# Recutting the last 128 tokens of a fused SSM and feed-forward kernel: pieces of 256, 128 and 128 columns against 416 and 96

## Chip, cores, metric

The kernel runs on one core of one Trainium2 chip. The metric is device time in microseconds, as the median of several executions.

## The reference, cut to what matters

```python
xn = layernorm(x)                          # x: 2048 tokens x 512, bf16
h  = scan over tokens of a diagonal complex SSM driven by xn
y  = x + 2*Re(h @ C.T) + xn*Dskip + (silu(xn @ w_gate) * (xn @ w_up)) @ w_down
```

The last matmuls into y contract over 1376 feed-forward rows and over the real and imaginary parts of 512 SSM states. In the kernel these are 19 passes of up to 128 rows into one PSUM bank for each block of 128 tokens.

## The kernel before

The 2048 tokens are four chunks of 512, each four blocks ("lt") of 128 tokens. For each block, ten passes of the feed-forward product (A) and nine more (B: one of left-over feed-forward rows, eight of SSM states, tile `hss`) gather in a PSUM bank. VectorE then adds the residual held in `x_sb`, and SyncE issues a store. Instructions are recorded as tasks with what they read and write. TensorE keeps the program's order; VectorE's order is chosen by a list scheduler that goes by the length of what depends on a task.

```python
def dc_chunk(c, mid=None, split_last=False):
    items = []
    for lt in range(4):
        if split_last and lt == 3:         # only in the last chunk
            items += [(lt, 0, 256), (lt, 256, 128), (lt, 384, 128)]
        else:
            items.append((lt, 0, 512))
    prs = [next_pair() for _ in range((len(items) + 1) // 2)]   # pairs of PSUM banks, 4 in all
    for (lt, c0, nc_), bk in zip(items, banks):
        ...                                # A: 10 matmuls of nc_ columns, hT x wd
    for (lt, c0, nc_), bk in zip(items, banks):
        ...                                # B: 9 matmuls of nc_ columns, hL x wd and hss x W12
        ...                                # VectorE: x_sb[:, a, c0:c0+nc_] += pbank[:, bk, 0:nc_]
        if nc_ == 128 and c0 == 256:
            continue
        d0, dn = (256, 256) if nc_ == 128 else (c0, nc_)
        dma(..., out_v[:, a, d0:d0 + dn], x_sb[:, a, d0:d0 + dn], ...)
```

## Time and profile before

| | before |
|---|---|
| three runs, us | 178.62, 179.29, 179.01 |
| span of the profiled run, us | 177.02 |
| TensorE busy, its share of the chain | 98%, 98% |
| VectorE busy | 92% |

In the profile lines, PE is TensorE, PEld its weight loads, DVE VectorE, SPq and ACTq the issues of stores by SyncE and ScalarE; xN counts the instructions in a line, and what stands behind <- ended the wait before them. The chain is the work that ended last, followed back from the end. A store lands when its completion is signalled.

The second is VectorE's order in that stretch (timeline: start, length, what, and how many):

```profile
161.71 1.28 DVE L985 TENSOR_TENSOR x_sb<-pb,x_sb 128x512 bf16<-128x512 f32 x2
162.90 2.36 DVE L914 TENSOR_TENSOR hss<-rot 128x2048 bf16<-128x2048 bf16 x2
165.17 1.23 DVE L612 TENSOR_TENSOR xn_sb<-xn_sb,dsk 128x2048 bf16<-128x2048 bf16 x1
```

Two adds of the chunk before stand ahead of the last writes of `hss`, which the last chunk's B needs.

### The profile page before, as it was taken

The numbers are of one execution on the slowest core, as the hardware profiler recorded it, in microseconds if no ns is written. First come the engines' busy times: TensorE is split into PE (matmuls) and PEld (weight loads), VectorE is DVE, ScalarE is ACT, GpSimd is POOL, SyncE is SP. The second block draws the span as 40 slices with busy tenths as digits, with TensorE's granted clock in tenths as the row PEclk, the third lists the DMA queues.
The fourth block names the chain that finished last, engine by engine and source line by source line (L and its number), as shares of the span: only waits on it lengthen the run. The fifth ranks groups of instructions, "written<-read, shape, count | busy, mean of one in ns | idle before, by whom it ended". The sixth has DMA issues, their size and how long they took to land.

```text
span 177.0 us, 2416 instructions
## 1 busy us (share of the span) xinstructions
PE 173.3 (98%) x927; PEld 84.0 (47%) x935; DVE 162.8 (92%) x283; ACT 87.4 (49%) x116; POOL 11.0 (6%) x22
## 2 busy tenths in 40 slices
PE   8999999999999999999999999999999999999994
PEld 3894444444444444444444444444444444444644
DVE  2975999899999999999999999999999999999943
ACT  4689989989999579220455554000366520000000
POOL 3040500055000000000000000000000000000000
DMA  5891694755675200002000000001100000000032
GB/s 167 280 373 61 142 126 104 252 120 118 118 255 140 46 0 0 0 4 89 31 0 0 0 0 4 0 0 59 59 0 4 0 0 0 0 0 33 30 111 67
DMA packets 22966, 12.37 MB, mean 70 GB/s; under 512 B 15180, under 2 KB 22956, under 8 KB 22956
## 3 DMA queue, kind: packets, MB, share of 16 engines
q1 hardware_dynamic: 22652, 11.77, 24.7%
q10 hardware_dynamic: 304, 0.46, 0.8%
q8 instruction: 7, 0.11, 0.3%
q14 instruction: 3, 0.02, 0.0%
HBM read 6.46 MB, written 2.10 MB: 48 GB/s over the span
## 4 chain that ended last, share of the span: by engine, by line
PE 98%; issue 0%; DVE 0%
PE pb L762 36%; PE pb L966 19%; PE pb L883 16%; PE pb L980 16%; PE pb L806 4%; PE pb L478 3%; PE pb L977 2%; PE pb L845 2%; PE pb L855 1%; PE pb L585 1%; DVE x_sb L985 0%
## 5 line engine op out<-in xcount | busy, mean ns | idle before, releaser
L923 DVE TENSOR_TENSOR_SCAN rot<-sm,car,rot 128x512 bf16<-128x512 f32 x32 | 38.7, 1266 | 0.0
L774 ACT ACTIVATE sg<-pb 128x1024 bf16<-128x1024 f32 x20 | 20.1, 1023 | 32.7 <-PE pb L762 32.0
L966 PE MATMUL pb<-wd,hT 128*128 128x512 bf16 (+2 forms) x176 | 34.5, 355 | 0.3 <-ACT uf L870 0.2
L980 PE MATMUL pb<-W,hss 128*128 128x512 bf16 (+2 forms) x140 | 29.6, 354 | 0.2
L762 PE MATMUL pb<-xnT,wu 128*128 128x512 bf16 x120 | 27.9, 379 | 0.0
L966 PEld LDWEIGHTS pb<-wd,hT 128*128 128x128 bf16 x180 | 16.8, 98 | 18.2 <-issue 0.4
L832 ACT ACTIVATE uf<-pb 128x1024 bf16<-128x1024 f32 x20 | 20.5, 1025 | 7.7 <-PE pb L762 7.4
L762 PE MATMUL pb<-xnT,wg 128*128 128x512 bf16 x92 | 21.8, 380 | 0.0
L883 PE MATMUL pb<-xnT,BT 128*128 128x512 bf16 x96 | 21.0, 379 | 0.0
L980 PEld LDWEIGHTS pb<-W,hss 128*128 128x128 bf16 x144 | 13.4, 97 | 14.4
L890 ACT ACTIVATE u_sb<-pb 128x1024 bf16<-128x1024 f32 x16 | 16.3, 1018 | 5.2 <-PE pb L883 5.2
L762 PEld LDWEIGHTS pb<-xnT,wu 128*128 128x128 bf16 x120 | 11.7, 98 | 14.2 <-ACT sg L774 0.2
L883 PEld LDWEIGHTS pb<-xnT,BT 128*128 128x128 bf16 x96 | 9.4, 98 | 11.3
L985 DVE TENSOR_TENSOR x_sb<-pb,x_sb 128x512 bf16<-128x512 f32 (+2 forms) x18 | 11.1, 630 | 3.7 <-PE pb L980 3.0
L762 PEld LDWEIGHTS pb<-xnT,wg 128*128 128x128 bf16 x92 | 9.0, 98 | 10.6
L834 DVE TENSOR_TENSOR hT<-sg,uf 128x1024 bf16<-128x1024 bf16 x20 | 13.4, 680 | 0.4 <-ACT uf L832 0.3
L483 DVE BATCH_NORM_STATS2 st<-x_sb 128x6 f32<-128x512 bf16 x12 | 7.5, 680 | 2.7 <-DMA x_sb<-in_A_x_dram 2.7
L914 DVE TENSOR_TENSOR rot<-u_sb,cosT 128x2048 bf16<-128x2048 bf16 x8 | 9.8, 1219 | 0.0
L914 DVE TENSOR_TENSOR rot<-rot,sin 128x2048 bf16<-128x2048 bf16 x8 | 9.8, 1219 | 0.0
L914 DVE TENSOR_TENSOR rot<-u_sb,sin 128x2048 bf16<-128x2048 bf16 x8 | 9.7, 1217 | 0.0
L914 DVE TENSOR_TENSOR rot<-rot,cosT 128x2048 bf16<-128x2048 bf16 x8 | 9.7, 1215 | 0.0
L914 DVE TENSOR_TENSOR rot<-rot 128x2048 bf16<-128x2048 bf16 x8 | 9.6, 1219 | 0.0
(93 smaller groups left out, 180.7 us busy)
## 6 DMA issues: line engine op xcount, KB each, us to landing
out_dram<-x_sb SPq DMA_DIRECT2D x15, 128.0 KB, 1.7
x_sb<-in_A_x_dram SPq DMA_DIRECT2D x3, 512.0 KB, 4.5
wd<-in_B_w_down_dram SPq DMA_DIRECT2D x1, 1280.0 KB, 6.2
wu<-in_B_w_up_dram SPq DMA_DIRECT2D x1, 768.0 KB, 4.7
wu<-in_B_w_up_dram SPq DMA_DIRECT2D x1, 608.0 KB, 6.8
x_sb<-in_A_x_dram SPq DMA_DIRECT2D x4, 128.0 KB, 3.2
wg<-in_B_w_gate_dram SPq DMA_DIRECT2D x1, 480.0 KB, 5.6
wg<-in_B_w_gate_dram ACTq DMA_DIRECT2D x1, 448.0 KB, 3.8
```

The source lines that it names most:

```text
L483: return g.add("dve", lambda e, a=a: e.bn_stats(out=st[:, a % 8, :], in_=x_sb[:, a, :]), reads=[("x", a)], writes=[("st", a % 8), ("st0", ...
L762: inst = e.matmul(pbank[0:fs, bk, :].rearrange("p (j t) -> p j t", j=4), lhsT=w[:, kt, i * 128:i * 128 + fs], rhs=xnT[c][:, :, kt, :], sta ...
L774: g.add("act", lambda e: e.activation(out=sg[rows, sl, 0:n, :].rearrange("p a t -> p (a t)"), in_=pair_f32(rows, bk, 512 * n), func=AF.Sil ...
L832: g.add("act", lambda e: e.activation(out=uf[rows, ul, 0:n, :].rearrange("p a t -> p (a t)"), in_=pair_f32(rows, bk, 512 * n), func=AF.Ide ...
L834: g.add("dve", lambda e: e.tensor_tensor(out=hT[rows, hb, i0:i0 + n, :], in0=sg[rows, sl, 0:n, :], in1=uf[rows, ul, 0:n, :], op=ALU.mult), ...
L883: inst = e.matmul(pbank[:, bk, :].rearrange("p (j t) -> p j t", j=4), lhsT=BT[:, ri, kt, pt * 128:(pt + 1) * 128], rhs=xnT[c][:, :, kt, :] ...
L890: g.add("act", lambda e: e.activation(out=u_sb[:, us].rearrange("p r t -> p (r t)"), in_=pair_f32(slice(0, 128), b0), func=AF.Identity), r ...
L914: tt = lambda out, a, b, op, r, w, nm: g.add("dve", lambda e: e.tensor_tensor(out=out, in0=a, in1=b, op=op), reads=r, writes=w, name="%s_% ...
L923: g.add("dve", lambda e, A0=A0, A1=A1, k=k, ri=ri, pt=pt: e.tensor_tensor_scan(out=A1[:, k, ri, :], data0=rr[:, pt:pt + 1].to_broadcast([1 ...
L966: inst = e.matmul(pbank[:, bk, 0:nc_], lhsT=hT[0:fs, hb, i, lt * 128:(lt + 1) * 128], rhs=wd[0:fs, i, c0:c0 + nc_], start=(i == 0), stop=F ...
L980: inst = e.matmul(pbank[:, bk, 0:nc_], lhsT=hss[:, hb, pt, ri, lt * 128:(lt + 1) * 128], rhs=W12[:, ri, pt, c0:c0 + nc_], start=False, sto ...
L985: g.add("dve", lambda e, bk=bk, a=a, c0=c0, nc_=nc_: e.tensor_tensor(out=x_sb[:, a, c0:c0 + nc_], in0=pbank[:, bk, 0:nc_], in1=x_sb[:, a, ...
```

## The change

The intent: what comes after the last matmul (an add, a store, its completion) can't be hidden, so make the last piece small, and put enough matmul work behind the big piece to cover its own add and store. The diff, cut to its core (it also drops the argument `mid`):

```diff
-                    items.append((lt, 0, 256))
-                    items.append((lt, 256, 128))
-                    items.append((lt, 384, 128))
+                    items.append((lt, 0, 416))
+                    items.append((lt, 416, 96))
...
-            for (lt, c0, nc_), bk in zip(items, banks):
+            def add_A(lt, c0, nc_, bk):
                 def mmA(e, ...):           # unchanged
...
+            for it, bk in zip(items, banks):
+                if it[2] >= 256:
+                    add_A(*it, bk)
             for (lt, c0, nc_), bk in zip(items, banks):
                 a = 4 * c + lt
+                if nc_ < 256:
+                    add_A(lt, c0, nc_, bk)
...
-                if nc_ == 128 and c0 == 256:
-                    continue
-                d0, dn = (256, 256) if nc_ == 128 else (c0, nc_)
-                dma("st_out%d_%d" % (a, d0), out_v[:, a, d0:d0 + dn], ...)
+                dma("st_out%d_%d" % (a, c0), out_v[:, a, c0:c0 + nc_], ...)
```

More of the change, by code (lines that the diff above doesn't have):

```diff
@@ L947, in ssm_elem_chunk, with dc_chunk @@
                     g.add("dve", lambda e, t2_=t2_, t4_=t4_, q_=q_: e.tensor_tensor(out=car[:, c + 1, 1, q_], in0=t4_, in1=t2_, op=ALU.add), reads=[("sm", "ct4", ph), ("sm", "ct2", ph)], writes=[("car", c + 1, ph)], name="c6_%d_%d" % (c, ph), est=70)
-        def dc_chunk(c, mid=None, split_last=False):
+        def dc_chunk(c, split_last=False):
             hb = c % 2
@@ L969, in dc_chunk @@
                       writes=BK(bk), name="mm_dA%d_%d" % (4 * c + lt, c0), est=FL * (216 if nc_ == 512 else nc_ * 0.43), ninst=FL)
-            if mid is not None:
-                mid()
+            for it, bk in zip(items, banks):
+                if it[2] >= 256:
+                    add_A(*it, bk)
             for (lt, c0, nc_), bk in zip(items, banks):
                 a = 4 * c + lt
+                if nc_ < 256:
+                    add_A(lt, c0, nc_, bk)
                 def mmB(e, bk=bk, lt=lt, hb=hb, c=c, c0=c0, nc_=nc_):
@@ L986, in dc_chunk @@
                       reads=BK(bk) + [("x", a)], writes=[("xo", a, c0)], name="oadd%d_%d" % (a, c0), est=(660 if nc_ == 512 else 100 + nc_))
-                if nc_ == 128 and c0 == 256:
-                    continue
-                d0, dn = (256, 256) if nc_ == 128 else (c0, nc_)
-                dma("st_out%d_%d" % (a, d0), out_v[:, a, d0:d0 + dn], x_sb[:, a, d0:d0 + dn], writes=[("out", a, d0)], nbytes=TILEB * dn // 512,
-                    reads=[("xo", a, c) for c in ((256, 384) if nc_ == 128 else (c0,))], out_=True)
+                dma("st_out%d_%d" % (a, c0), out_v[:, a, c0:c0 + nc_], x_sb[:, a, c0:c0 + nc_], writes=[("out", a, c0)], nbytes=TILEB * nc_ // 512,
+                    reads=[("xo", a, c0)], out_=True)
         ffn_gate_quarters([0, 1, 2, 3])
```

## The prediction

> **What bounds the kernel now.** I read the page first: engine shares, then the chain of work that ended last.
>
> ```profile
> PE 173.3 (98%) x927; PEld 84.0 (47%) x935; DVE 162.8 (92%) x283; ACT 87.4 (49%) x116; POOL 11.0 (6%) x22
> ...
> PE 98%; issue 0%; DVE 0%
> ```
>
> TensorE is the chain from first to last; VectorE, at 92%, is near it but never on it before the last add. So for most of the span only TensorE's passes count. The change touches only the end, so next came the chain of the last microseconds (start, length, what):
>
> ```profile
> 170.71 0.22 PE pb L977
> 170.92 1.73 PE pb L980 x8
> 172.65 0.11 PE pb L977
> 172.76 0.88 PE pb L980 x8
> 173.64 0.06 PE pb L977
> 173.69 0.45 PE pb L980 x8
> 174.15 0.06 PE pb L977
> 174.20 0.46 PE pb L980 x8
> 174.66 0.02 issue
> 174.69 0.29 DVE x_sb L985
> ```
>
> This gives the true cost of a pass, which the groups' durations hide because matmuls overlap. Nine B passes (one of L977, eight of L980) are 170.71 to 172.65 = 1.94 us at 512 columns, 216 ns each; 172.65 to 173.64 = 0.99 us at 256, 110 ns each; 173.64 to 174.15 = 0.51 us at 128, 56.7 ns each. All three are columns x 0.4167 ns plus about 3 ns. The last pass is over at 174.66, the last add runs to 174.98, and about 2.0 us of store and completion follow up to the span's 177.0. Next the groups by shape in the last stretch:
>
> ```profile
> L980 PEld LDWEIGHTS pb<-W,hss 128*128 128x128 bf16 x60 | 5.3, 97 | 4.4
> ...
> L985 DVE TENSOR_TENSOR x_sb<-pb,x_sb 128x512 bf16<-128x512 f32 x7 | 4.6, 688 | 2.5 <-PE pb L980 2.5
> ...
> L985 DVE TENSOR_TENSOR x_sb<-pb,x_sb 128x128 bf16<-128x128 f32 x2 | 0.6, 292 | 0.3 <-PE pb L980 0.2
> L985 DVE TENSOR_TENSOR x_sb<-pb,x_sb 128x256 bf16<-128x256 f32 x1 | 0.4, 425 | 0.3 <-PE pb L980 0.3
> ```
>
> The adds cost 292, 425 and 688 ns for 128, 256 and 512 columns: about 1.03 ns a column on about 160 ns. VectorE stands idle for TensorE before these last adds, so it isn't behind. Last the stores, in the stretch 174.9 to 177 (40 slices of 52.5 ns, then the issues in it):
>
> ```profile
> DMA  0479963000000000005999520000000000000000
> ...
> out_dram<-x_sb SPq DMA_DIRECT2D x1, 64.0 KB, 1.6
> ```
>
> Two bursts: the 64 KB store of columns 0 to 255, issued at 174.13, and the last 64 KB store, issued at 175.01, whose data flow from about 175.8 to 176.16. So 0.8 us pass before data move, 0.37 us with them, 0.45 us to the landing at about 176.6. A 128 KB store (issued 171.46) moves its data in about 0.6 us, read the same way in a wider stretch. SyncE spends 0.33 us on each issue.
>
> **What the Trainium skill says.** "TensorE: Matmul & The Clock Gate", section Back-to-back issue gap, gives N/2.4 + 2.5 ns for matmuls alone (55.8 ns at N=128), yet says that a stream of weight loads and matmuls sustains only about 81 ns at N=128. This trace has such a stream at 56.7, so here the first form holds and the 81 doesn't. The same page, LDWEIGHTS (loading the stationary operand), gives columns / 1.2, 107 ns for 128 columns; the trace's records say 97 ns, but successive ones start every 57 ns in the 128-column pieces, so a record's length isn't what a load occupies. How far below 57 ns it can go, no line shows. "VectorE: DVE Perf Modes", section on the TRN2 errata, gives (N + 151) / 0.96 ns for an fp32 tensor add: 291, 424 and 691 ns at 128, 256 and 512, and the trace's adds from PSUM agree within 3 ns. "DMA: Bandwidth & Descriptors", Specifications, puts the least size for full rate at 512 B and says that smaller writes are done by read-modify-write. All stores of the kernel before have rows of 512 B or 1 KB, so this trace can't say what a 192 B row costs.
>
> **The change part by part.** Every column of the last 128 tokens needs 19 passes: 10 in A, 9 in B.
>
> 1. Passes. Before: 19 x (110 + 56.7 + 56.7) = 19 x 223.4 = 4.24 us. After: 416 columns at 416 x 0.4167 + 3.4 = 176.7 ns; 96 columns, if they stream, at 40 + 3.4 = 43.4 ns: 19 x 220.1 = 4.18 us. Gain 0.06 us. Columns are the same; 19 pass overheads go.
>
> 2. Order. Ten passes of the last piece leave the A block, which then costs 10 x 176.7 rather than 10 x 223.4: B of chunk 3 starts 0.47 us earlier, 166.34 in place of 166.81. This needs hss by then: its last write ends at 165.26. So no new wait, and nothing gained either, since the passes return at the end. The 416 piece then ends at 172.65 - 0.47 + 9 x 0.1767 = 173.77, and the last piece at 173.77 + 19 x 0.0434 = 174.60 (before 174.66). The 19 passes, 0.82 us, cover the 416 add (425 + 160 x 1.03 = 590 ns, 173.80 to 174.39), so VectorE is free when they end.
>
> 3. Last add: 96 columns, 292 - 32 x 1.03 = 259 ns (the skill's form: 257), 0.03 us less. It ends near 174.89.
>
> 4. Stores. The 416 store (104 KB) is issued at about 174.42; SyncE is free again at 174.75, before the last store is wanted at 174.92. By 0.6 us for 128 KB and 0.37 for 64, I estimate 0.51 us of data for 104 KB (175.2 to 175.7) and 0.23 for 24 KB, starting at about 175.7: they just miss each other. The last store saves 0.37 - 0.23 = 0.14 us if bytes rule; it has as many rows, 128, and rows under 512 B, so I count 0.10.
>
> Sum: 0.06 + 0.03 + 0.10 = 0.19 us off the end, the best plain case: 179.01 - 0.19 = 178.82. Everything before 164 us stays, give or take the order of VectorE: the adds of chunk 2 whose banks are used again no longer stand before the A block in the dependencies, so the list scheduler may place them later and the hss work earlier. The adds have ample room, as VectorE has 1.26 us of idle before the add at 170.74.
>
> **The rivals.** First, weight loads bound the 96-column passes. If a load and its matmul can't go faster than the 57 ns seen at 128 columns, the piece costs 19 x 56.7 = 1.08 us, 0.25 more than reckoned, and the sum becomes a loss of 0.06 us: 179.07. For it: each pass has its own load, no pass here is shorter than 57 ns, and 97 ns records overlap already. Against: the spacing at 128 fits the plain column law to within a nanosecond, so nothing but streaming shows there. If the skill's 81 ns were a floor, 19 x 81 = 1.54 us would cost 0.7 more (179.5), but 56.7 has been seen, so hardly. I give a bound somewhere between 43 and 57 ns about two chances in five.
>
> Second, the store doesn't shrink. The 192 B rows may each pay a read-modify-write or a fixed price, and the last burst may queue behind the 416 store on the same engines. Then the 0.10 is nil or turns into a loss of 0.1 to 0.2: 178.9 to 179.1. For it: the skill's 512 B line, the two bursts nearly touching, and landings of 1.5 to 1.7 us that barely move with size, 64 against 128 KB. Against: a burst is only a fifth of the landing anyway, so it can't grow by much.
>
> Third, the reordered VectorE delays something earlier: hss late for B, or the 416 add late so that the last add queues. Room is 166.34 - 165.26 = 1.1 us for the first, 174.63 - 174.39 = 0.24 us for the second. Should it fail, it costs tenths, near 179.3. One in ten.
>
> **Range and chances.** 178.82 with three chances in five, near 179.0 with the rest, rivals two and three leaning up: I predict 178.9. All terms are tenths, while the three runs before lie between 178.62 and 179.29, so scatter sets the range: 178.4 to 179.4. A 2% change would be 3.6 us; the whole tail after the last pass is 2.3 us and most of it is fixed, so faster by over 2% has 1%, slower 1%, within 2% has 98%.
>
> **What would show each step.** Passes: the chain's last nine to nineteen passes at 43 ns each (right), at 50 to 57 (first rival). Order: B of chunk 3 starting near 166.3 with no wait for VectorE. Add: a group of 96 columns near 259 ns and one of 416 near 590, the last add's idle ended by TensorE. Stores: issues of 104 and 24 KB half a microsecond apart, the latter landing in 1.5 us or less; 1.7 or more would be the second rival. The prediction would be wrong if TensorE waited anywhere in the last 20 us, if the passes of 96 columns took over 60 ns, or if the small store's landing took 2 us.

## More of the kernel before

All executions quoted here are of granted TensorE clock 0.998 to 1.000.

The prediction reads most of this profile. Two readings are added here, as they serve for comparing. The first is the start of the last chunk's A passes in the chain of the kernel before (start, length, what):

```profile
158.13 5.18 PE pb L966 x24
```

From there to the span's end are 177.02 - 158.13 = 18.89 us. I call this **the end stretch**.

## The result, and the profile after

The changed kernel took 178.77 us (median of 6, 178.61 to 179.07), the kernel before in the same rounds and earlier 179.16 us (6 runs, 178.62 to 179.40). The ratio is 0.9983, with a 95% interval of 0.9966 to 1.0. Ratios are the mean time of one kernel's fast runs over that of the other's of the same rounds, so not quite the ratio of the medians.

The chain of the changed kernel, to set against that of before (L980 and L983 are the former L977 and L980, L988 the former L985):

```profile
158.16 8.23 PE pb L966 x40
166.40 0.22 PE pb L980
...
172.24 0.18 PE pb L980
172.41 1.41 PE pb L983 x8
173.82 0.42 PE pb L966 x10
174.25 0.04 PE pb L980
174.29 0.36 PE pb L983 x8
174.65 0.02 issue
174.67 0.26 DVE x_sb L988
```

The piece of 416 columns is done at 173.82, then ten A and nine B passes of the last piece follow in 0.83 us, 43.7 ns each. The groups by shape in the last 20 us show the two adds:

```profile
L988 DVE TENSOR_TENSOR x_sb<-pb,x_sb 128x416 bf16<-128x416 f32 x1 | 0.6, 591 | 0.9 <-PE pb L983 0.9
...
L988 DVE TENSOR_TENSOR x_sb<-pb,x_sb 128x96 bf16<-128x96 f32 x1 | 0.3, 258 | 0.2 <-PE pb L983 0.2
```

Both waited for TensorE; neither found VectorE still busy. The DMA view from 174.9 to 177, in the same slices of 52.5 ns as that of before:

```profile
DMA  0000000068999841047741000000000000000000
...
out_dram<-x_sb SPq DMA_DIRECT2D x1, 24.0 KB, 1.5
```

The first burst is the 104 KB store, the second the 24 KB store, with hardly a gap between them; the landing is 1.5 us in place of 1.6. VectorE's order did change (timeline):

```profile
159.52 2.36 DVE L914 TENSOR_TENSOR hss<-rot 128x2048 bf16<-128x2048 bf16 x2
...
165.33 1.28 DVE L988 TENSOR_TENSOR x_sb<-pb,x_sb 128x512 bf16<-128x512 f32 x2
```

`hss` is complete at 161.88 in place of 165.26, and the two adds have moved behind it. TensorE waited for neither, before or after.

The end stretch went from 18.89 to 18.72 us (176.88 - 158.16). The trace's own times, not yet rounded, cut it into its parts (so a difference can be 0.01 off what the lines above give):

| part of the end stretch, us | before | after | difference |
|---|---|---|---|
| first A pass to the last pass's end | 16.54 | 16.49 | -0.05 |
| to the end of the last add | 0.32 | 0.28 | -0.035 |
| to the last store's issue | 0.03 | 0.03 | 0 |
| issue to the end of its data | 1.17 | 1.09 | -0.09 |
| end of data to the end of the span | 0.84 | 0.84 | 0 |
| sum | 18.89 | 18.72 | -0.17 |

(Rows are rounded one by one.)

### The profile page after: what moved, and what is told of

Its sections match the earlier page's. It is cut to its first block, busy times and chain, and to the rows that moved or that the text cites. A ratio compares the mean times of both kernels' runs of the same rounds, so it can differ in the third digit from the quotient of the medians.

```text
span 176.9 us, 2385 instructions
## 1 busy us (share of the span) xinstructions
PE 173.8 (98%) x916; PEld 82.7 (47%) x916; DVE 162.4 (92%) x282; ACT 87.3 (49%) x116; POOL 11.0 (6%) x22
## 4 chain that ended last, share of the span: by engine, by line
PE 98%; DVE 0%; issue 0%
PE pb L762 36%; PE pb L966 20%; PE pb L983 16%; PE pb L883 16%; PE pb L806 4%; PE pb L478 3%; PE pb L980 2%; PE pb L845 2%; PE pb L855 1%; PE pb L585 1%; DVE x_sb L988 0%
## 5 line engine op out<-in xcount | busy, mean ns | idle before, releaser
L966 PE MATMUL pb<-wd,hT 128*128 128x512 bf16 (+2 forms) x170 | 35.4, 367 | 0.0
L983 PE MATMUL pb<-W,hss 128*128 128x512 bf16 (+2 forms) x136 | 30.4, 366 | 0.0
L966 PEld LDWEIGHTS pb<-wd,hT 128*128 128x128 bf16 x170 | 16.0, 97 | 19.0 <-ACT scrC L730 0.4
L983 PEld LDWEIGHTS pb<-W,hss 128*128 128x128 bf16 x136 | 12.9, 97 | 14.9
L988 DVE TENSOR_TENSOR x_sb<-pb,x_sb 128x512 bf16<-128x512 f32 (+2 forms) x17 | 10.9, 655 | 3.5 <-PE pb L983 3.2
```

The source lines that it names most:

```text
L966: inst = e.matmul(pbank[:, bk, 0:nc_], lhsT=hT[0:fs, hb, i, lt * 128:(lt + 1) * 128], rhs=wd[0:fs, i, c0:c0 + nc_], start=(i == 0), stop=F ...
L983: inst = e.matmul(pbank[:, bk, 0:nc_], lhsT=hss[:, hb, pt, ri, lt * 128:(lt + 1) * 128], rhs=W12[:, ri, pt, c0:c0 + nc_], start=False, sto ...
L988: g.add("dve", lambda e, bk=bk, a=a, c0=c0, nc_=nc_: e.tensor_tensor(out=x_sb[:, a, c0:c0 + nc_], in0=pbank[:, bk, 0:nc_], in1=x_sb[:, a, ...
```

## The experiments

All kernels gave correct results. For each there is one profile, and times beside the kernel before on the same chip. A difference of 0.1 us in the time is below what so few runs resolve; the end stretch repeats far better (18.72 in both traces of the changed kernel and in that of adds_pulled_early, which ends alike). The kernel before has one trace; old_split_late, whose parts and stores are the same, gives 18.90. The medians are from five sets of rounds, in which the kernel before had 179.16, 179.23, 179.15, 178.81 and 179.14, so they compare within a set only; each ratio is to the kernel before of its own set. All results first, sorted by the end stretch:

| kernel | end stretch, us | median, us (runs) | ratio to before (95%) |
|---|---|---|---|
| changed kernel | 18.72 | 178.77 (6) | 0.9983 (0.9966 to 1.0) |
| again | 18.72 | 178.84 (6) | 0.9985 (0.9966 to 1.0003) |
| adds_pulled_early | 18.72 | 178.69 (4) | 0.9984 (0.9956 to 1.0011) |
| after_two_queues | 18.73 | 178.85 (4) | 0.9985 (0.9970 to 0.9999) |
| last_store_64k | 18.81 | 179.10 (6) | 0.9989 (0.9973 to 1.0005) |
| before | 18.89 | 179.16 (6) | 1 |
| old_split_late | 18.90 | 179.24 (6) | 0.9996 (0.9979 to 1.0014) |
| split_440_72 | 18.97 | 179.14 (4) | 1.0005 (0.9989 to 1.0022) |
| split_256_256 | 18.98 | 178.97 (4) | 0.9993 (0.9972 to 1.0015) |
| a_in_front_two_queues | 19.04 | 179.07 (4) | 1.0005 (0.9985 to 1.0026) |
| split_440_72_two_queues | 19.11 | 178.97 (4) | 1.0008 (0.9977 to 1.0038) |
| a_in_front | 19.15 | 179.23 (6) | 0.9998 (0.9983 to 1.0014) |
| split_480_32 | 19.28 | 179.28 (4) | 1.0014 (0.9990 to 1.0038) |
| one_piece | 19.33 | 179.33 (4) | 1.0017 (0.9994 to 1.0040) |

My theory was the prediction's sum: slightly less streaming, a smaller last add, a smaller last store, and an order that keeps the 416 add and store clear of them. The rivals were that the order or VectorE's rescheduling alone does it, that the short rows of the last store cost what they save, or that the difference is scatter.

### again: the changed kernel unaltered

> The changed kernel unaltered. If the prediction's sum holds (0.06 us of passes, 0.03 us of add, 0.10 us of store), it is 0.1 to 0.3 us below the kernel before in the mean. The rival, that the 0.39 us between the first medians was scatter, puts it within 0.05 us. The profile should again show the 19 last passes in 0.83 us, a last add of 258 ns and a last landing of 1.5 us.

The median was 178.84 us against 179.23 for the kernel before, ratio 0.9985. The end stretch was again 18.72, with the 19 passes in 0.83 us, an add of 258 ns and a landing of 1.5 us. The interval of the time just includes 1, so this run alone doesn't exclude scatter; that three more measurements with this ending (the first one, adds_pulled_early and after_two_queues) all gave 0.9983 to 0.9985 speaks against it, and the stretch shows where the time went.

### a_in_front: the new pieces without the new order

```diff
-                if it[2] >= 256:
+                if it[2] >= 0:
                     add_A(*it, bk)
...
-                if nc_ < 256:
+                if nc_ < 0:
                     add_A(lt, c0, nc_, bk)
```

> The split of 416 and 96, but all A passes in front as before. Theory: the order is what hides the add of 416. Only 9 passes of 43.5 ns, 0.39 us, then lie between the end of the 416 piece and the end of the last one, less than its 591 ns of add. TensorE ends at the same time, the last add starts about 0.2 us after TensorE's end in place of 0.02, and the span is 0.2 us longer than the changed kernel's, about that of the kernel before. Rival: the order is idle, and the end does not move.

The end stretch was 19.15 us, 0.43 longer than the changed kernel's: the order matters, but twice as much as I expected. From this kernel's timeline, the last B passes and the adds:

```profile
174.30 0.50 PE L983 MATMUL pb<-W,hss 128*128 128x96 bf16 x8
174.45 0.76 DVE L988 TENSOR_TENSOR x_sb<-pb,x_sb 128x416 bf16<-128x416 f32 x2 [0.90 <-PE pb L983]
```

And its stores' issues after 174.8 (fastest, median and slowest in ns, then first and last start):

```profile
L405 SPq DMA_DIRECT2D out_dram<-x_sb x2: 332/382/431, 175.1 to 175.4; - x2
```

The 416 add starts only 0.36 us before TensorE signals its last pass (174.82), so the two adds run back to back to 175.21. That is 0.39 us after the signal, against 0.28 in the changed kernel: 0.11 us lost. Then comes what I had left out: SyncE is busy with the 416 store's issue, so the last one starts at 175.45 and not at 175.24 (0.21 us lost), and an issue that had to queue takes 0.43 us rather than 0.33 (0.10 more). Together 0.11 + 0.21 + 0.10 = 0.42, the whole difference but for rounding.

### old_split_late: the new order without the new pieces

```diff
-                    items.append((lt, 0, 416))
-                    items.append((lt, 416, 96))
+                    items.append((lt, 0, 256))
+                    items.append((lt, 256, 128))
+                    items.append((lt, 384, 128))
```

The stores are those of the kernel before.

> The old pieces of 256, 128 and 128 with the old stores, but the A passes of the two small pieces moved behind the B of the 256 piece, each piece's own A and B together. Theory: the order alone is worth nothing where the adds had room anyway, so the tail after the last pass (last add 292 ns, landing 1.6 us of 64 KB) is that of the kernel before, and the time is within 0.1 us of it. Rival: the order itself, or the list scheduler's other order of VectorE, brings the gain, 0.2 us or more.

The end stretch was 18.90 us against 18.89, the ratio 0.9996. The order alone is worth nothing; with old pieces it had nothing to uncover. Neither half of the change gains by itself: the new pieces in the old order (a_in_front) lost 0.25 us against the kernel before, and both together gained 0.17.

### last_store_64k: the small piece with a large last store

```diff
-                dma("st_out%d_%d" % (a, c0), out_v[:, a, c0:c0 + nc_], ...)
+                d0, dn = {416: (0, 256), 96: (256, 256)}.get(nc_, (c0, nc_))
+                dma("st_out%d_%d" % (a, d0), out_v[:, a, d0:d0 + dn], ...)
```

> The changed kernel with its passes and adds, but the stores cut at column 256: the first of columns 0 to 255 after the 416 add, the last of columns 256 to 511 (64 KB, rows of 512 B) after the 96 add. Theory: the last burst is 0.37 us in place of 0.23, the landing 1.6 in place of 1.5, so the end comes 0.10 to 0.14 us later than in the changed kernel. Rival: rows of 192 B cost as much as they save, and the end stays or comes earlier.

The end stretch was 18.81 us, 0.09 longer than the changed kernel's, with passes, adds and moments of issue as there, which is just under the range given. The landing was read as 1.5 us, not 1.6, so at one decimal that view can't carry it; the time from issue to the end of the data can: 1.18 us here, 1.09 in the changed kernel, 1.17 before. So the smaller last store, with its shorter rows, is worth 0.09 us. Short rows took less time in all: a packet (one row) of 192 B took 15 ns in the median, one of 512 B 27 ns and one of 832 B 39 ns. They took more for each byte: the 24 KB moved at 98 GB/s (0.25 us), 64 KB at 187 GB/s (0.35 us).

### split_480_32: how short can a pass be?

```diff
-                    items.append((lt, 0, 416))
-                    items.append((lt, 416, 96))
+                    items.append((lt, 0, 480))
+                    items.append((lt, 480, 32))
```

> Pieces of 480 and 32 columns. It asks how short a pass with its own weight load can be. If passes only stream, the last 19 are 32 x 0.4167 + 3.4 = 16.7 ns apart, 0.32 us in all; if a load or an issue sets a floor, they are 25 ns apart or more, 0.48 us or more, and TensorE ends 0.16 us or more later than in the changed kernel. Either way the 480 add (about 657 ns) outlasts the 19 passes, the last add of about 191 ns waits for VectorE, and the end is about 0.2 us later than in the changed kernel, in spite of the smaller last add and an 8 KB store.

From its timeline, the last eight passes and their weight loads:

```profile
174.54 0.27 PEld L983 LDWEIGHTS pb<-W,hss 128*128 128x128 bf16 x8
174.57 0.35 PE L983 MATMUL pb<-W,hss 128*128 128x32 bf16 x8
```

One of these matmuls is recorded with 176 ns, so the eight starts are (350 - 176) / 7 = 25 ns apart; the loads too, (270 - 97) / 7. That is longer than streaming (16.7 ns), and equals the floor of 25 ns that the Trainium skill gives for matmuls in "TensorE: Matmul & The Clock Gate", section Back-to-back issue gap. A weight load for each pass doesn't raise it. So weight loads did not bound the 96-column passes, which need 43.7 ns.

The end stretch was 19.28 us, 0.56 longer than the changed kernel's, where I had said 0.2. Again the last store was issued 0.38 us after the one before it, at 175.55, although the last add was over at 175.25, and again that issue took 0.43 us. Of the 0.56 us, 0.16 is the floor of the passes (TensorE ended that much later, as expected), 0.28 the wait for SyncE, and 0.12 the adds, the longer issue and the completion. What I had left out is again the queue on SyncE.

### split_256_256 and one_piece: the sizes

The edits are the pieces, (0, 256) and (256, 256) with the test changed so that the second goes behind the first, and (0, 512).

> Two halves of 256 columns, the second's 19 passes behind the first's. Theory: last add 424 ns in place of 258 (0.17 us more) and a last store of 64 KB (0.10 us more), passes 19 x 220 ns as in the changed kernel: the end 0.27 us after the changed kernel's and within 0.1 us of the kernel before. Rival: only the number of pieces counts, and it equals the changed kernel.

> The last 128 tokens in one piece of 512, as all others. Theory: passes 19 x 216.7 ns (0.06 us less than in the changed kernel), last add 688 ns (0.43 more), last store 128 KB with a landing of 1.7 us (0.2 more): 0.55 to 0.6 us longer than the changed kernel. Rival: the tail's pieces hardly matter, within 0.2 us.

The end stretches were 18.98 us, 0.26 above the changed kernel (expected 0.27), and 19.33, 0.61 above (expected 0.55 to 0.6). Their last adds took 425 and 691 ns. Both rivals fall, and the sum of add and store holds over a wide range of sizes. These kernels also isolate the passes: with the last tokens in one, two and three pieces (19, 38 and 57 passes; one_piece, split_256_256 or the changed kernel, old_split_late or before), TensorE ended 16.43, 16.49 and 16.54 us after the first A pass. Each 19 passes more cost 0.05 us, about 2.7 ns a pass.

### adds_pulled_early: VectorE's old order

The A passes of the 416 piece are made to depend on two adds of the chunk before, so that the scheduler puts these early.

```diff
-                g.add("pe", mmA, reads=[("hT", hb, i) for i in range(FL)] + [("wd", 0)],
+                g.add("pe", mmA, reads=[("hT", hb, i) for i in range(FL)] + [("wd", 0)] + ([("xo", 8, 0), ("xo", 9, 0)] if nc_ == 416 else []),
```

> The changed kernel, but the A passes of the 416 piece are made to depend on the first two adds of chunk 2, so that the list scheduler puts these adds early on VectorE, as in the kernel before; their stores then go out some 4 us earlier. Theory: VectorE has over 0.7 us of idle before the adds that count, so nothing moves at the end, within 0.1 us of the changed kernel. Rival: the other order of VectorE is a part of the gain, and the time goes back by 0.1 us or more or TensorE shows a wait.

The adds went early again, ahead of the `hss` work, and the end stretch stayed at 18.72 us. VectorE's reordering is harmless and worthless here.

### a_in_front_two_queues: SyncE's share of a_in_front

```diff
-                    reads=[("xo", a, c0)], out_=True)
+                    reads=[("xo", a, c0)], out_=True, eng="act" if (a == 15 and c0 > 0) else "sp")
```

(and the end of the kernel waits for that store as well; A in front as in a_in_front).

> As a_in_front, but the last store is issued from ScalarE, which is idle by then, in place of SyncE. a_in_front was 0.43 us longer than the changed kernel from the first A pass of chunk 3 to the end (19.15 against 18.72 us), twice what was expected: its last add ended 0.11 us later after TensorE's end, but the last store was issued only when SyncE had done the 416 store's issue, and that issue took 0.43 in place of 0.33 us. Theory: the queueing on SyncE is the rest; with the second queue the stretch falls to 18.85 to 18.95. Rival: two stores of the same rows so close in time slow each other in the DMA engines or at their landing, and the stretch stays near 19.1.

The stretch was 19.04 us: a tenth shorter than 19.15, but above the range. The last two stores (as in the tile view of `out_dram`):

```profile
L405 SPq DMA_DIRECT2D out_dram<-x_sb x1: 332/332/332, 175.0 to 175.0; - x1
L405 ACTq DMA_DIRECT2D out_dram<-x_sb x1: 366/366/366, 175.2 to 175.2; - x1
...
DMA to landing us min/median/max: 1.7/1.7/1.7
```

The issue did move: it began at 175.16, 0.20 us earlier when counted from the first A pass, and took 0.37 us. So SyncE's queueing is a part. But the last store's data then overlapped those of the 416 store by 0.16 us, and half of those 0.20 us was lost again: 0.04 in the time from issue to the end of the data, 0.07 from there to the end. Both theories are partly right.

### split_440_72_two_queues: a finer cut

> The changed kernel with pieces of 440 and 72 and the last store issued from ScalarE. The 440 add takes 615 ns, 19 passes of 33.4 ns take 635, so it just fits; the last add takes 232 ns in place of 258, the store is 18 KB, and no issue waits for another. Theory: the stretch is 18.65 to 18.72 us, 0 to 0.07 below the changed kernel's 18.72, not to be seen in the time. Rival: an issue from ScalarE is slower or two queues disturb each other, and the stretch is longer by 0.1 us or more.

The add only nearly fits (617 ns; it ended 0.03 us after the last pass, and the last add followed at once), the last add took 233 ns, and the last store was issued at 174.86, by the stretch 0.03 us earlier than in the changed kernel. Yet the stretch was 19.11 us. For its two stores, first the one from SyncE, then the one from ScalarE, the time from issue to landing:

```profile
L405 SPq DMA_DIRECT2D out_dram<-x_sb x1: 333/333/333, 174.6 to 174.6; - x1
L405 ACTq DMA_DIRECT2D out_dram<-x_sb x1: 366/366/366, 174.9 to 174.9; - x1
...
DMA to landing us min/median/max: 1.9/1.9/1.9
```

Both landed 1.9 us after their issue, where the changed kernel's take 1.7 and 1.5. The data of the last were over at 176.02, only 0.05 later in the stretch than in the changed kernel, but the span ended 1.18 us after that, in place of 0.84. The rival held: issuing closer bought nothing, and 0.34 of the 0.39 us lost lie behind the end of the data.

### after_two_queues and split_440_72: queue or closeness?

after_two_queues is the changed kernel with the ScalarE issue; split_440_72 has the finer cut with SyncE alone.

> The changed kernel (416 and 96) with the last store issued from ScalarE. In split_440_72_two_queues the last store was issued 0.24 us after the one before and its data ended about when they do in the changed kernel, but the span ended 1.18 us after the data in place of 0.84. Theory A, closeness: it is the nearness of the two stores that delays completion; here they are issued about 0.48 us apart as in the changed kernel, so the stretch from the first A pass of chunk 3 to the end is 18.70 to 18.80 us. Theory B, the queue: completion of a store from ScalarE's queue is slow of itself, and the stretch is 18.9 or more.

> Pieces of 440 and 72, both stores from SyncE. The 440 issue (0.33 us) ends about 0.09 us after the last add is done, so the last store waits for it and, as in a_in_front, takes about 0.43 us to issue: 0.1 to 0.25 us longer than the changed kernel's stretch of 18.72, so 18.82 to 18.97. If SyncE's queueing did not matter, it would be 18.65 to 18.72.

With 0.48 us between the two issues, the second queue cost nothing (18.73 us), so it isn't ScalarE's queue that lands slowly. With the finer cut on SyncE, the last issue came 0.38 us after the one before and took 0.43 us, and the stretch was 18.97, at the upper end of the range. So in these runs 0.48 us between the last two issues cost nothing, on one queue or on two, and every smaller distance cost something: 0.38 us on SyncE a longer issue, 0.17 and 0.24 us on two queues a later completion. Why completion came later isn't settled: it was seen strongly in one kernel with one profile, and weakly in a_in_front_two_queues (0.91 us after the data). Theory A isn't shown by this. In a_in_front_two_queues the issues were closer still (0.17 against 0.24 us) and the data overlapped by the same 0.16 us, yet its stores landed 1.7 us after their issue, not 1.9. Closeness alone therefore doesn't explain the 1.9; a second profile of split_440_72_two_queues would show whether it repeats.

No cut that I tried beats the changed kernel by the end stretch; adds_pulled_early and after_two_queues, with the same cut, are level with it.

## Why the prediction was right

- **Passes.** Predicted 0.06 us less, measured 0.05, and 0.05 again for each 19 passes in the kernels with other pieces. The 96-column pass was put at 43.4 ns and took 43.7. The first rival (a load-bound pass of up to 57 ns, held at two chances in five) was wrong: at 32 columns a pass with its load goes every 25 ns.
- **Order.** B of the last chunk was put at 166.34 and began at 166.40, with no wait. That the 416 add ends before the last passes do was right (0.22 us of idle for the last add), and that SyncE is free in time was too (at 174.81, 0.15 us before the last issue); a_in_front and split_480_32 show that the second is the tighter of the two. What an overlap costs was missed in my later expectations, not in the prediction.
- **Last add.** Predicted 259 ns, measured 258. The step from the last pass to the add's end fell by 0.035 us, against 0.03.
- **Store.** Predicted 0.10 us less, measured 0.09, both in the change and when the large store was put back. The working was less exact than its sum. The prediction read 0.6 us for the data of 128 KB from a view with wide slices, where the trace's packets took 0.52, and 0.37 for 64 KB, where they took 0.34. So its bursts, estimated at 0.51 and 0.23 us, took 0.45 and 0.25, and the discount from 0.14 to 0.10 us was a guess that fitted. That the bursts just miss each other was partly luck: the first began at 175.31, and with 0.51 us it would have run into the second, at 175.79. The time from the data to the landing was read as 0.45 us from a rounded landing; it is 0.38. The second rival (short rows that eat the saving) didn't come.
- **VectorE's order.** It was foreseen, and adds_pulled_early shows that it costs and brings nothing.
- **Sum.** 0.19 us as the best plain case, 0.17 in the end stretch. The range given, 178.4 to 179.4, would have held no change at all (179.16), so the median within it says little; the parts carry the account. The prediction of 178.9 leaned upwards for rivals that didn't come; the medians were 178.77 and 178.84, and the ratios stand for about 0.3 us less than before (179.16 x 0.0017). The tenth by which the times exceed the stretch isn't explained. It is within the intervals, and the start of the last chunk alone varies by half a microsecond between traces.

## What to carry to other kernels

The unhidden end of a kernel is last pass, last add, last issue, last data and completion; a smaller last piece shortens only the add (1.03 ns a column here) and the data. Choose the last piece so that its matmul passes, moved whole behind the piece before it, cover that piece's add, and look at the time between the last two stores' issues: with 0.48 us they cost nothing here, while the finer cuts, with 0.24 to 0.38 us, lost 0.25 to 0.56 us, more than the change had gained. When an effect is a thousandth of the time, measure a stretch of the trace that begins after the scatter.

## What the Trainium skill lacked or had wrong

- "TensorE: Matmul & The Clock Gate", section Back-to-back issue gap, says that a stream of weight loads and matmuls sustains about 81 ns at N=128 and 131 at N=512. Here such streams ran at 216 ns for 512 columns, 56.7 for 128, 43.7 for 96 and 25 for 32; the page's figures for matmuls alone, floor of 25 ns included, hold within 1.2 ns with a load for each.
- The same page, section LDWEIGHTS, gives 107 ns for 128 columns. Loads of that shape started every 25 ns in split_480_32, while each was recorded with 95 to 98 ns, so the formula isn't the spacing of loads in a stream. The page's section on weight-path perf modes does allow faster loads for 128 columns of bf16; which mode ran, no run here shows.
- "DMA: Bandwidth & Descriptors", section Specifications, puts the least size for full rate at 512 B. That agrees in direction: 128 rows of 192 B moved at 98 GB/s, 128 rows of 512 B in split_256_256 at 187 GB/s. But no step showed at 512 B, nor a later completion: packets of 64, 192, 512, 832 and 1024 B took 11, 15, 27, 39 and 46 ns in the median, within 1 ns of 8.7 ns plus 0.0365 ns a byte (a line laid through these five), so fewer bytes in as many rows still saved time.
- The same page, section Issuing engines are not separate DMA queues, calls the time that the sequencer takes to issue usually small relative to the DMA itself. Here it was 0.33 us on SyncE, 0.43 when it followed at once on another issue, and 0.37 on ScalarE: about a quarter of the last store's 1.46 us from issue to landing, and more than its data took (0.25 us). I found no figure on the page for how much later stores land when their data overlap (1.9 us each in place of 1.7 and 1.5 in split_440_72_two_queues, but 1.7 each in a_in_front_two_queues).
